# The scale of V in a fused attention and gated-MLP kernel: maximum over partitions through DRAM and VectorE in place of TensorE

## The chip, the cores and the metric

The kernel runs on one NeuronCore of one Trainium2 chip. The metric is the device time of one execution in microseconds; 649.65 us is the median of three runs of the kernel before (648.05 to 651.03). The engines are named as in the profile: PE is TensorE's matmuls and PEld its weight loads, DVE is VectorE, ACT is ScalarE, POOL is GpSimd, and SP is the engine whose queue issues every DMA of this kernel. Each engine takes its instructions strictly in the order in which the program put them.

## The reference, cut to what matters

Eight batches, eight heads, 576 positions, head dimension 64, float32. Attention looks back at most 127 positions, so a tile of 128 queries meets two tiles of 128 keys.

```python
scores = scale * np.matmul(q, k.transpose(0, 1, 3, 2))
scores = np.where(mask, scores + bias[None], -1000000000.0)   # 0 <= i - j < 128, a slope per head
attn = np.exp(scores - max)
attn = attn / (sum + 1e-09)
out = np.matmul(attn, v)
x = out.transpose(0, 2, 1, 3).reshape(B, S, H * D)
h = np.maximum(x @ w_in, 0.0)
u, v = h[..., :512], h[..., 512:]
v_n = (v - mu) / np.sqrt(var + 1e-06)
v_s = w_spatial @ v_n + b_spatial
return (u * v_s) @ w_out
```

## The kernel before, in words

Work comes in blocks and units. An attention block is one batch and two heads, 32 blocks in all; five of them (batch 0 and the first of batch 1) run in another way, `raw_tile`, and are not touched. The other 27 run in `attention`: scores on PE (L520: eight matmuls for the first four query tiles, then two for the last; the profile counts each of these float32 matmuls twice), bias and minimum on DVE (L531), exponential with row sums on ACT (L537), a reciprocal (L545, L549), two float16 halves of the probabilities (L557 on ACT, L562 on DVE), one DMA transpose for each head (L568, on SP), and probabilities times V on PE in float16 (L624, 84 matmuls). ACT and DVE then copy the result out of PSUM as two float32r parts (L633, L637), with a small copy of the last 64 columns (L267).

For the float16 product V is scaled by a power of two and split into `vh` and `vl`. The scale comes from the largest row sum of |V|: ACT takes the sums of 128 partitions (L579, into column 0 of `am`; its wide output goes to `vl`, which is free then). PE transposes the 128 sums into one row (L583), DVE takes the maximum and clamps it (L587, L588), and PE spreads it to all partitions by two matmuls of one column with constant powers of two (L593). DVE reads the two columns from PSUM and keeps their exponents (L599, L600). Column 5 of `am` then scales V (L604 on DVE or L607 on ACT, and L611), column 6 scales the result back (L633, L637).

The gated MLP of a batch is made of units of one PSUM tile each: v units (L689, 12 matmuls of 512 columns; L711 for the last 64 positions), with a layer norm behind them (L650 to L700); u units (L741, 12 matmuls of 288 columns), spatial units (L762, 14) with L770 and L776 on DVE behind them, and output units (L788, 12) with a copy (L267) and a store (L798). All their matmuls are float32r; those of L520 and L583 are float32, L593 is bfloat16, L624 float16. The tiles `m` of these units have two buffers, the tiles `x` (L624's result, and the little tile `mp` of L583 and L593) two, `vh`, `vl` and `am` two.

The order on every engine is written by a planner (class `Plan`). Every operation has an engine, an estimated length and a due time; the planner runs these through a list schedule with a fixed latency for each engine (2200 ns for a DMA) and emits the program in that order. So an operation with other estimates moves others, on every engine. The attention blocks of a batch stand among the units of the batch before.

Of the kernel before, what the change touches and what calls it, by code (L numbers as in the profile page):

```python
# [9 lines left out]
F32 = mybir.dt.float32  # L10
F32R = mybir.dt.float32r
BF16 = mybir.dt.bfloat16
F16 = mybir.dt.float16
I32 = mybir.dt.int32
U32 = mybir.dt.uint32
AF = mybir.ActivationFunctionType
ALU = mybir.AluOpType
AX = mybir.AxisListType
# [120 lines left out]
def attn_gmlp_kernel(ctx, tc, qk, v, w_in, w_spT, b_sp, w_out, outT):  # L139
# [3 lines left out]
    nc = tc.nc  # L143
    B, H, D, _, S = qk.shape
    P = 2 * D
# [22 lines left out]

    const = ctx.enter_context(tc.tile_pool(name="const", bufs=1))
    work = ctx.enter_context(tc.tile_pool(name="work", bufs=2))  # L170
    ps = ctx.enter_context(tc.tile_pool(name="ps", bufs=1, space=PSUM))
    ctx.enter_context(tc.manual_schedule())
    plan = Plan()

    def fixed(shape, dtype, name):
        t = const.tile(shape, dtype, name=name)
        return Buf(lambda: t)

    def dve(n, fast=False):
        return 75 + n / (1.92 if fast else 0.96)  # L180
# [13 lines left out]

    nhalf = fixed([P, 1], F32, "nhalf")
    ident = fixed([P, P], F32, "ident")
    ones = fixed([1, 2 * P], BF16, "ones")
    tabs = [fixed([P, 2 * P], BF16, f"tab{h}") for h in range(H)]
    win = fixed([P, NC_, 2, DF], F32R, "win")
    wout = fixed([P, ND, 2, DM], F32R, "wout")  # L200
# [23 lines left out]
    def constants():  # L224
        def f():
            nc.gpsimd.iota(relf(), [[-1, 2 * P]], base=P, channel_multiplier=1, allow_small_or_imprecise_dtypes=True)
        plan.add("POOL", 400, 0, f, (), [(relf, 0)])

        def f():
            nc.vector.memset(maskt(), 0.0)  # L230
        plan.add("DVE", dve(256), 0, f, (), [(maskt, 0)])

        def f():
            nc.gpsimd.affine_select(maskt(), maskt(), [[-1, 2 * P]], ALU.is_ge, MASKED, base=P, channel_multiplier=1)
            nc.gpsimd.affine_select(maskt(), maskt(), [[1, 2 * P]], ALU.is_ge, MASKED, base=-1, channel_multiplier=-1)
        plan.add("POOL", 800, 1, f, [(maskt, 0)], [(maskt, 0)])

        def f():
            nc.vector.memset(ident(), 1.0)
            nc.vector.memset(ones()[:, :P], 2.0 ** -12)  # L240
            nc.vector.memset(ones()[:, P:], 2.0 ** -13 / PSC)
            nc.vector.memset(nhalf(), -0.5)
            nc.vector.memset(rstat(), 1.0)
        plan.add("DVE", dve(400), 500, f, (), [(ident, 0), (ones, 0), (nhalf, 0)] + [(rstat, k) for k in range(8)])

        def f():
            nc.gpsimd.affine_select(ident(), ident(), [[-1, P]], ALU.is_ge, 0.0, base=0, channel_multiplier=1)
            nc.gpsimd.affine_select(ident(), ident(), [[1, P]], ALU.is_ge, 0.0, base=0, channel_multiplier=-1)
        plan.add("POOL", 600, 500, f, [(ident, 0)], [(ident, 0)])

        def f():
            nc.vector.tensor_scalar(minus(), ident(), -1.0, None, ALU.mult)
        plan.add("DVE", 150, 501, f, [(ident, 0)], [(minus, 0)])
        for j in range(2):
            def f(j=j):
                nc.vector.memset(stat[j](), 1.0)
            plan.add("DVE", dve(64), 600, f, (), [(stat[j], x) for x in range(99)])
        for h in range(H):
            def f(h=h):
                slope = 2.0 ** (-8.0 * (h + 1) / H)  # L260
                nc.vector.scalar_tensor_tensor(tabs[h](), relf(), -8.0 * slope, maskt(), ALU.mult, ALU.add)
            plan.add("DVE", dve(256), 1000 + h * 4000, f, [(relf, 0), (maskt, 0)], [(tabs[h], 0)])
# [237 lines left out]
    def attention(b, p):  # L500
# [70 lines left out]

        vh, vl = (plan.buf(work, tag, 2, [P, NQ, P], F16) for tag in ("vh", "vl"))
        am = plan.buf(work, "am", 2, [P, 8], F32)
        one = plan.buf(work, "one", 2, [1, 2], BF16)
        mp = plan.buf(ps, "x", 2, [P, 512], F32)
        d = due - 3000

        def f():
            nc.scalar.activation(vl(), vr(), AF.Abs, accum_out=am()[:, 0:1])  # L579
        plan.add("ACT", act(NQ * P, 1), d, f, VRS, [(vl, 0), (am, 0)])  # L580

        def f():
            nc.tensor.transpose(mp()[0:1, 0:P], am()[:, 0:1], ident())  # L583
        plan.add("PE", SWITCH // 2, d + 1, f, [(am, 0), (ident, 0)], [(mp, 0)])

        def f():
            nc.vector.tensor_reduce(one()[:, 0:1], mp()[0:1, 0:P], AX.X, ALU.max)  # L587
            nc.vector.tensor_scalar(one()[:, 0:1], one()[:, 0:1], 2.0 ** -98, 2.0 ** 126, ALU.max, ALU.min)  # L588
        plan.add("DVE", 400, d + 2, f, [(mp, 0)], [(one, 0)])

        def f():
            for k in range(2):
                nc.tensor.matmul(mp()[:, P + k:P + k + 1], ones()[:, k * P:(k + 1) * P], one()[:, 0:1], start=True, stop=True,  # L593
                                 skip_group_check=True)
        plan.add("PE", SWITCH, d + 3, f, [(one, 0), (ones, 0)], [(mp, 1)])

        def f():
            bits = 0x7F800000
            nc.vector.tensor_scalar(am()[:, 5:7].bitcast(I32), mp()[:, P:P + 2].bitcast(I32), bits, None, ALU.bitwise_and)  # L599
            nc.vector.tensor_scalar(am()[:, 5:6].bitcast(I32), am()[:, 5:6].bitcast(I32), bits, None, ALU.bitwise_xor)  # L600
        plan.add("DVE", 150, d + 4, f, [(mp, 1)], [(am, 1)])

        def fv():
            nc.vector.tensor_scalar(vh(), vr(), am()[:, 5:6], None, ALU.mult)  # L604
# [268 lines left out]
```

## Time and profile before

| What | Value |
|---|---|
| Runs | 648.05, 651.03, 649.65 us; median 649.65 us |
| Profiled execution | 648.05 us |
| Its span, first to last instruction | 646.3 us |
| Granted TensorE clock, mean | 0.992 |
| PE busy | 619.0 us (96%) |
| DVE busy | 524.2 us (81%) |
| ACT busy | 430.9 us (67%) |
| One batch in the steady part (375.78 to 448.74 us) | 72.96 us |

Busy time of PE is the time in which some matmul was under way; matmuls are pipelined, so a group's length says less than the distance from its start to the start of what follows. Rows of the timeline give the start, the length, the engine, the line, the operation, the tiles and the count; in brackets stands the idle time before it and what ended it.

### The profile page before, as it was taken

What the parts mean: (1) busy time and instruction counts of PE and PEld (TensorE: products, weight loads), DVE (VectorE), ACT (ScalarE), POOL (GpSimd) and SP (SyncE); (2) the same over time, 40 slices, a digit from 0 to 9 for tenths busy, and PEclk for the clock granted to TensorE, in tenths of its full rate; (3) what the DMA queues carried; (4) which work ended last, traced back from release to release, by engine and by line L of the source; (5) the groups of instructions that cost most, each with busy time, mean ns of one, the idle gap of its engine ahead of it and who ended that gap; (6) DMA issues with size and microseconds to landing.
All of it is one profiled execution on the core that took longest, in us unless ns stands there. A gap on an engine that the chain in (4) does not pass through costs nothing.

```text
span 646.3 us, 14141 instructions
## 1 busy us (share of the span) xinstructions
PE 619.0 (96%) x5037; PEld 529.8 (82%) x5037; DVE 524.2 (81%) x1897; ACT 430.9 (67%) x1322; POOL 29.6 (5%) x53
## 2 busy tenths in 40 slices
PE   4879999999999999999999999999999999999997
PEld 2445688778899879988898979988898978988997
DVE  6999898999887979887887979887887979873632
ACT  4698675989585848686686848676686857662211
POOL 1000010000200010000100010000100010000100
PEclk9998799999999999999999999999999999999999
DMA  7903013799156863778165753858166751733001
GB/s 264 329 20 130 19 62 119 169 209 202 55 132 133 190 107 93 155 155 184 40 143 127 191 112 89 154 152 188 32 154 125 193 113 10 132 79 76 2 20 55
DMA packets 149291, 79.34 MB, mean 123 GB/s; under 512 B 128610, under 2 KB 139874, under 8 KB 149220
## 3 DMA queue, kind: packets, MB, share of 16 engines
q1 hardware_dynamic: 149220, 78.44, 51.8%
q8 instruction: 39, 0.64, 0.4%
q14 instruction: 32, 0.26, 0.1%
HBM read 37.13 MB, written 9.44 MB: 72 GB/s over the span
## 4 chain that ended last, share of the span: by engine, by line
PE 79%; DVE 17%; issue 1%; DMA 1%; ACT 1%; SPq 1%; ACTq 0%; DVEq 0%
PE m L762 16%; PE m L741 16%; PE m L788 14%; PE m L689 13%; PE s L520 8%; PE x L624 6%; DVE pq L562 4%; PE m L711 2%; DVE prob L436 2%; DVE prob L531 2%; DVE gs L298 1%; DMA pt<-in_qk_dram 1%; DVE prob L450 1%; DVE u L770 1%; DVE o L267 1%
## 5 line engine op out<-in xcount | busy, mean ns | idle before, releaser
L537 ACT ACTIVATE prob<-prob,stat 128x128 f32<-128x128 f32 (+1 forms) x270 | 125.4, 466 | 13.6 <-DVE stat L531 12.4
L762 PE MATMUL m<-wsp,vn 128*128 128x288 f32 x768 | 124.3, 299 | 0.7 <-DVE u L770 0.7
L788 PE MATMUL m<-gs,wout 128*128 128x288 f32 x768 | 113.5, 301 | 0.3 <-DVE gs L776 0.2
L762 PEld LDWEIGHTS m<-wsp,vn 128*128 128x128 f32 x768 | 107.5, 188 | 6.7 <-issue 1.9
L557 ACT ACTIVATE pq<-prob,stat 128x128 f16<-128x128 f32 x270 | 103.1, 464 | 12.7 <-ACT prob L537 10.2
L741 PE MATMUL m<-xt,win 128*128 128x288 f32 x768 | 111.6, 298 | 0.0
L788 PEld LDWEIGHTS m<-gs,wout 128*128 128x128 f32 x768 | 103.3, 188 | 7.2 <-issue 1.7
L562 DVE SCALAR_TENSOR_TENSOR pq<-prob,stat,pq 128x128 f16<-128x128 f32 x270 | 104.0, 437 | 4.3 <-ACT pq L557 3.7
L741 PEld LDWEIGHTS m<-xt,win 128*128 128x128 f32 x768 | 103.9, 188 | 4.1 <-issue 2.3
L689 PE MATMUL m<-win,xt 128*128 128x512 f32 x384 | 93.5, 396 | 1.7 <-DVE o L267 1.7
L531 DVE CUSTOM_DVE_ANT_0 prob<-s,tab 128x128 f32<-128x128 f32 (+1 forms) x270 | 89.2, 376 | 2.6 <-PE s L520 2.1
L689 PEld LDWEIGHTS m<-win,xt 128*128 128x128 f32 x384 | 71.5, 189 | 18.2 <-DVE o L267 2.8
L520 PE MATMUL s<-qkraw 64*128 64x256 f32 (+2 forms) x540 | 66.5, 360 | 1.5 <-DVE stat L531 1.3
L770 DVE TENSOR_TENSOR u<-m,u 128x288 f32<-128x288 f32 x64 | 28.9, 451 | 34.2 <-PE m L762 34.2
L520 PEld LDWEIGHTS s<-qkraw 64*128 64x128 f32 (+1 forms) x540 | 42.0, 175 | 16.2 <-issue 9.0
L659 POOL TENSOR_TENSOR st<-st,nhalf 128x1 f32<-128x1 f32 (+1 forms) x40 | 25.6, 640 | 560.4 <-DVE st L655 548.0
L537 ACT ACTIVATION_READ_ACCUMULATOR prob<-prob,stat 128x1 f32 x270 | 50.6, 187 | 0.0
L267 ACT COPY o<-m 128x288 f32<-128x288 f32 x37 | 14.6, 395 | 46.2 <-PE m L788 45.9
L624 PE MATMUL x<-pt,vh 128*64 128x256 f16 (+6 forms) x756 | 41.7, 229 | 0.0
L271 ACT ACTIVATE vt<-m 128x512 f32<-128x512 f32 x31 | 18.5, 598 | 33.0 <-DVE st L654 16.1
L637 DVE SCALAR_TENSOR_TENSOR xt<-x,am,xt 128x288 fp32r<-128x288 f32 x54 | 26.2, 507 | 17.1 <-ACT xt L633 17.0
L624 PEld LDWEIGHTS <-vh 128*64 128x64 f16 x756 | 31.7, 110 | 5.8 <-issue 3.5
(132 smaller groups left out, 820.7 us busy)
## 6 DMA issues: line engine op xcount, KB each, us to landing
qkraw<-in_qk_dram SPq DMA_DIRECT2D x28, 576.0 KB, 3.9
out_dram<-o SPq DMA_DIRECT2D x64, 144.0 KB, 2.0
vraw<-in_v_dram SPq DMA_DIRECT2D x28, 320.0 KB, 2.9
vn<-in_w_in_dram SPq DMA_DIRECT2D x6, 512.0 KB, 7.1
pt<-in_w_out_dram SPq DMA_DIRECT2D x4, 512.0 KB, 4.5
gs<-in_w_spT_dram SPq DMA_DIRECT2D x4, 288.0 KB, 5.0
xt<-in_w_in_dram SPq DMA_DIRECT2D x2, 512.0 KB, 6.8
qkraw<-in_qk_dram SPq DMA_DIRECT2D x3, 320.0 KB, 8.3
```

The costliest lines, as they stand in the source:

```text
L520: nc.tensor.matmul(sc[k][j]()[:m, i, :k1 - k0], raw()[rows, 0, t * P:t * P + m], raw()[rows, 1, k0:k1], start=True, stop=True)
L531: nc.vector.tensor_tensor_reduce(pt(), sc()[:m, i, :n], tabs[h]()[:m, c0:c0 + n], -0.125, 3e38, ALU.add, ALU.min, st()[:m, NM, j, t:t + 1])
L537: nc.scalar.activation(pt(), pt(), AF.Exp, bias=st()[:m, NM, j, t:t + 1], scale=-1.0, accum_out=st()[:m, SM, j, t:t + 1])
L557: nc.scalar.activation(pq[j]()[:m, 0, cs], prob[j]()[:m, cs], AF.Copy, scale=st()[:m, RC, j, t:t + 1])
L562: nc.vector.scalar_tensor_tensor(pq[j]()[:m, 1, cs], prob[j]()[:m, cs], st()[:m, RC, j, t:t + 1], pq[j]()[:m, 0, cs], ALU.mult, ALU.subtract)
L624: nc.tensor.matmul(xp()[j * D:(j + 1) * D, x0:x0 + n], l()[:, kt, j * D:(j + 1) * D], rhs[:, o:o + n], start=j not in seen, stop=False, sk ...
L637: nc.vector.scalar_tensor_tensor(xt()[:, S + R + hf * HS:S + R + (hf + 1) * HS], xp()[:, :HS], am()[:, 6:7], xt()[:, qs].bitcast(F32), ALU ...
L689: nc.tensor.matmul(pt(), xt[c]()[:, X0[a] + t * P:X0[a] + (t + 1) * P], win()[:, c, w, DH:DF], start=(n == 0), stop=(n == 3 * NC_ - 1))
L741: nc.tensor.matmul(pt()[:, :HS], win()[:, c, w, d * P:(d + 1) * P], xt[c]()[:, X0[a] + hf * HS:X0[a] + (hf + 1) * HS], start=(n == 0), sto ...
L762: nc.tensor.matmul(pt()[:, :HS], l, r, start=(n == 0), stop=(n == len(ops) - 1))
L770: nc.vector.tensor_tensor(u(), pt()[:, :HS], u(), ALU.mult)
L788: nc.tensor.matmul(pt()[:, :HS], wout()[:, d, w, e * P:(e + 1) * P], gs[d]()[:, a, :], start=(n == 0), stop=(n == 3 * ND - 1))
```

## The change

The row sums go from column 0 of `am` to a DRAM tile of 128 words by one DMA (`row`), and from there to every partition by a second one, a broadcast of 512 bytes to each of 128 partitions, into the first 128 words of `vl` seen as float32. Both are issued on SP; the second waits for the landing of the first. DVE then does the rest on all 128 partitions: maximum, clamp, exponent bits, product with the two powers of two, and the flip of the exponent bits. The transpose, the two matmuls, the tile `mp`, the tile `one` and the constant row `ones` are gone; a constant of two columns (`powers`) takes its place. The arithmetic of the rest is the same.

```diff
+    dram = ctx.enter_context(tc.tile_pool(name="dram", bufs=2, space=bass.MemoryType.DRAM))
...
-            nc.vector.memset(ones()[:, :P], 2.0 ** -12)
-            nc.vector.memset(ones()[:, P:], 2.0 ** -13 / PSC)
+            nc.vector.memset(powers()[:, 0:1], 2.0 ** -12)
+            nc.vector.memset(powers()[:, 1:2], 2.0 ** -13 / PSC)
...
-        def f():
-            nc.tensor.transpose(mp()[0:1, 0:P], am()[:, 0:1], ident())
-        plan.add("PE", SWITCH // 2, d + 1, f, [(am, 0), (ident, 0)], [(mp, 0)])
-
-        def f():
-            nc.vector.tensor_reduce(one()[:, 0:1], mp()[0:1, 0:P], AX.X, ALU.max)
-            nc.vector.tensor_scalar(one()[:, 0:1], one()[:, 0:1], 2.0 ** -98, 2.0 ** 126, ALU.max, ALU.min)
-        plan.add("DVE", 400, d + 2, f, [(mp, 0)], [(one, 0)])
-
-        def f():
-            for k in range(2):
-                nc.tensor.matmul(mp()[:, P + k:P + k + 1], ones()[:, k * P:(k + 1) * P], one()[:, 0:1], start=True, stop=True,
-                                 skip_group_check=True)
-        plan.add("PE", SWITCH, d + 3, f, [(one, 0), (ones, 0)], [(mp, 1)])
+
+        row = plan.buf(dram, "row", 2, [P, 1], F32)
+        wide = lambda: vl().rearrange("p a b -> p (a b)").bitcast(F32)[:, :P]
+
+        def f():
+            nc.sync.dma_start(row(), am()[:, 0:1])
+        plan.add("SP", 60, d + 1, f, [(am, 0)], [(row, 0)])
+
+        def f():
+            nc.sync.dma_start(wide(), row().rearrange("p o -> (p o)").partition_broadcast(P))
+        plan.add("SP", 300, d + 2, f, [(row, 0)], [(vl, 0)])
 
         def f():
             bits = 0x7F800000
-            nc.vector.tensor_scalar(am()[:, 5:7].bitcast(I32), mp()[:, P:P + 2].bitcast(I32), bits, None, ALU.bitwise_and)
+            nc.vector.tensor_reduce(am()[:, 1:2], wide(), AX.X, ALU.max)
+            nc.vector.tensor_scalar(am()[:, 2:3], am()[:, 1:2], 2.0 ** -98, 2.0 ** 126, ALU.max, ALU.min)
+            nc.vector.tensor_scalar(am()[:, 2:3].bitcast(I32), am()[:, 2:3].bitcast(I32), bits, None, ALU.bitwise_and)
+            nc.vector.tensor_scalar(am()[:, 5:7], powers(), am()[:, 2:3], None, ALU.mult)
             nc.vector.tensor_scalar(am()[:, 5:6].bitcast(I32), am()[:, 5:6].bitcast(I32), bits, None, ALU.bitwise_xor)
-        plan.add("DVE", 150, d + 4, f, [(mp, 1)], [(am, 1)])
+        plan.add("DVE", 600, d + 4, f, [(vl, 0), (powers, 0)], [(am, 1)])
```

In the changed kernel lines up to the pool stand where they were; from there to the place of the change they are one higher (L520 is L521), behind it one lower (L624 is L623). The new lines are L586 (`row`), L590 (the broadcast) and L595 to L599 on DVE.

The planner moves the rest. The first place is PE, from the end of a steady batch's attention to the v units of the next batch. Before:

```order
L583 MATMUL x<-ident,am 1x128
L689 MATMUL m<-win,xt 128x512 x12
L593 LDWEIGHTS ones
L593 MATMUL x<-one,ones 128x1
L593 LDWEIGHTS ones
L593 MATMUL x<-one,ones 128x1
L711 MATMUL m<-win,xt 128x512 x8
L689 MATMUL m<-win,xt 128x512 x12
```

Ahead of these rows stand 24 matmuls of L788, and ahead of those the 84 of L624, the last block of the batch. Now (L623 is the last block's product, L521 the scores, L688 and L710 the v units):

```order
L623 LDWEIGHTS vl
L623 MATMUL x<-pt,vl 64x64
L521 MATMUL s<-qkraw 128x128 x2
L521 MATMUL s<-qkraw 128x256 x6
L688 MATMUL m<-win,xt 128x512 x12
L710 MATMUL m<-win,xt 128x512 x8
L688 MATMUL m<-win,xt 128x512 x36
```

The three instructions of the scale are gone here. The first v unit now stands one group of scores behind the product whose result it reads, where two output units stood between them, and three v units stand behind L710 where one did.

The second place is SP in the middle of a steady batch, where the two transposes of that last block are issued. `pq_85` and `pq_86` before, `pq_87` and `pq_88` now, are the same two tiles, one for each head. Before:

```order
L409 DMA qkraw<-in_qk_dram 128x1152
L798 DMA out_dram<-o 128x288
L411 DMA vraw<-in_v_dram 128x640
L568 DMA_TRANSPOSE pt<-pq_85 128x18x128
L568 DMA_TRANSPOSE pt<-pq_86 128x18x128
L409 DMA qkraw<-in_qk_dram 128x1152
```

Now:

```order
L797 DMA out_dram<-o 128x288
L412 DMA vraw<-in_v_dram 128x640
L586 DMA row<-am 128x1
L797 DMA out_dram<-o 128x288
L569 DMA_TRANSPOSE pt<-pq_87 128x18x128
L590 DMA vl<-row 128x128
L569 DMA_TRANSPOSE pt<-pq_88 128x18x128
L797 DMA out_dram<-o 128x288 x2
```

The second transpose now stands behind a DMA that waits for the landing of `row`.

The third place is DVE at the end of a steady batch, ahead of the copies of that block's result (L636 now, L637 before). Now:

```order
L268 COPY o<-m 128x288
L595 TENSOR_REDUCE am<-vl 128x1
L596 TENSOR_SCALAR am<-am 128x1
L597 TENSOR_SCALAR am<-am 128x1
L598 TENSOR_SCALAR am<-powers,am 128x2
L599 TENSOR_SCALAR am<-am 128x1
L532 ISA prob_86,stat_89<-s,tab_72 128x256
L532 ISA stat_89 128x1
L603 TENSOR_SCALAR vh<-vraw,am 128x640
L610 SCALAR_TENSOR_TENSOR vl<-vraw,am,vh 128x640
```

Behind them come L532, L546, L550 and three L563, and then L636. Before, the scale that comes next at this place (L587 and what follows it) stood behind the copies of this block; now a scale's five instructions and the split of another block's V stand ahead of them.

More of the change, by code (lines that the diff above doesn't have):

```diff
@@ L196, in attn_gmlp_kernel @@
     ident = fixed([P, P], F32, "ident")
-    ones = fixed([1, 2 * P], BF16, "ones")
+    powers = fixed([P, 2], F32, "powers")
     tabs = [fixed([P, 2 * P], BF16, f"tab{h}") for h in range(H)]
@@ L239, in f @@
             nc.vector.memset(ident(), 1.0)
-            nc.vector.memset(ones()[:, :P], 2.0 ** -12)
-            nc.vector.memset(ones()[:, P:], 2.0 ** -13 / PSC)
+            nc.vector.memset(powers()[:, 0:1], 2.0 ** -12)
+            nc.vector.memset(powers()[:, 1:2], 2.0 ** -13 / PSC)
             nc.vector.memset(nhalf(), -0.5)
             nc.vector.memset(rstat(), 1.0)
-        plan.add("DVE", dve(400), 500, f, (), [(ident, 0), (ones, 0), (nhalf, 0)] + [(rstat, k) for k in range(8)])
+        plan.add("DVE", dve(400), 500, f, (), [(ident, 0), (powers, 0), (nhalf, 0)] + [(rstat, k) for k in range(8)])
         def f():
@@ L573, in attention @@
         am = plan.buf(work, "am", 2, [P, 8], F32)
-        one = plan.buf(work, "one", 2, [1, 2], BF16)
-        mp = plan.buf(ps, "x", 2, [P, 512], F32)
         d = due - 3000
```

## The prediction

> **What bounds the kernel now.** I read the page first, then one steady batch, then what PE waits for.
>
> ```profile
> span 646.3 us, 14141 instructions
> ...
> PE 619.0 (96%) x5037; PEld 529.8 (82%) x5037; DVE 524.2 (81%) x1897; ACT 430.9 (67%) x1322; POOL 29.6 (5%) x53
> ```
>
> ```profile
> 375.78:448.74 72.96, 72.53 (x621) 63.56 (x621) 61.04 (x223) 52.13 (x164) 3.17 (x5) 1.00 0.58 133
> ...
> 435.00:445.00 10.00, 10.00 (x103) 9.06 (x101) 8.80 (x37) 9.69 (x34) 0.00 (x0) 1.00 0.79 182
> ```
>
> The columns of the second view are length, then busy time of PE, PEld, DVE, ACT and POOL. A steady batch lasts 72.96 us and PE is busy in 72.53 of them; DVE has 11.92 us free. So time taken off PE comes off the batch, as long as nobody makes PE wait. In the ten microseconds ahead of the next batch's v units, though, ACT (9.69 of 10) and DVE (8.80) are nearly full as well: there a delay has the least room. Of PE's own waits the summary has one that returns in every steady batch:
>
> ```profile
> PE m L689 <- DVE o L267: 1.7, 4, 0.4
> ```
>
> **The change: what leaves PE.** The price of a removed group is not its busy time, since matmuls overlap, but the distance between starts. PE in order of time (start, length, then the group):
>
> ```profile
> 423.95 1.86 PE L788 MATMUL m<-gs,wout 128*128 128x288 f32 x12
> 425.65 0.27 PE L583 MATMUL x<-ident,am 128*1 128x128 f32 x1
> 425.85 0.54 PE L520 MATMUL s<-qkraw 64*64 64x192 f32 x4
> 426.32 1.86 PE L788 MATMUL m<-gs,wout 128*128 128x288 f32 x12
> 428.11 0.20 PE L593 MATMUL x<-one,ones 1*128 1x1 bf16 x2
> 428.24 0.66 PE L762 MATMUL m<-wsp,vn 128*128 128x288 f32 x3
> ...
> 435.92 0.88 PE L520 MATMUL s<-qkraw 64*64 64x192 f32 x4
> 436.73 3.44 PE L788 MATMUL m<-gs,wout 128*128 128x288 f32 x24
> 440.10 0.41 PE L624 MATMUL x<-pt,vh 128*64 128x256 f16 x4
> ...
> 441.60 3.44 PE L788 MATMUL m<-gs,wout 128*128 128x288 f32 x24
> 444.88 0.27 PE L583 MATMUL x<-ident,am 128*1 128x128 f32 x1
> 445.58 3.03 PE L689 MATMUL m<-win,xt 128*128 128x512 f32 x12 [0.43 <-DVE o L267]
> 448.55 0.20 PE L593 MATMUL x<-one,ones 1*128 1x1 bf16 x2
> 448.67 2.11 PE L711 MATMUL m<-win,xt 128*128 128x512 f32 x8
> ...
> 460.68 1.79 PE L520 MATMUL s<-qkraw 64*128 64x128 f32 x16
> 462.40 1.85 PE L741 MATMUL m<-xt,win 128*128 128x288 f32 x12
> 464.09 0.27 PE L583 MATMUL x<-ident,am 128*1 128x128 f32 x1
> 464.12 1.84 PE L741 MATMUL m<-xt,win 128*128 128x288 f32 x12
> 465.89 0.54 PE L520 MATMUL s<-qkraw 64*64 64x192 f32 x4
> 466.37 0.20 PE L593 MATMUL x<-one,ones 1*128 1x1 bf16 x2
> 466.49 3.72 PE L741 MATMUL m<-xt,win 128*128 128x288 f32 x26
> ```
>
> The block at 464: L583 takes 0.03, the L741 behind it 1.77 where the one ahead takes 1.69 (0.08 more), L593 0.12: together 0.23. The block at 425: L583 takes 0.20 ahead of L520, L593 0.13, and the L788 that now borders on L593 takes 1.79, where one of the 24 at 436.73 takes 3.37 / 2 = 1.69 (0.10 more): 0.43. So a change of number format at a border costs about 0.1, and a scale in the middle of float32r units pays it more often than one beside L520. The other two blocks of a batch stand like the second (float32r units around L593) and I count them as 0.43. Mean (0.23 + 3 x 0.43) / 4 = 0.38 us, times 27 blocks = **10.3 us off PE**.
>
> The new order also takes two waits from their places. From L583 at 444.88 to L689 are 0.70 us where 0.03 is the price: 0.67 of waiting, 0.43 of it under the name of a copy out of PSUM (the tiles `m` have two buffers). Now other groups stand between that copy and the v unit. It came four times: 2.7 us. The L520 at 435.92 takes 0.81 where the one at 425.85 takes 0.47; it now stands elsewhere: 0.34 in five batches, 1.7 us. Upper bound of the gain: 10.3 + 2.7 + 1.7 = 14.7 us.
>
> **What is added to DVE.** Rows of the grouped view, one execution each:
>
> ```profile
> L587 DVE TENSOR_REDUCE one<-x 1x1 bf16<-1x128 f32 x27 | 7.4, 273 | 0.0
> L588 DVE TENSOR_SCALAR one<-one 1x1 bf16<-1x1 bf16 x27 | 3.9, 145 | 0.9
> L600 DVE TENSOR_SCALAR am<-am 128x1 int32<-128x1 int32 x27 | 4.2, 154 | 0.9
> L599 DVE TENSOR_SCALAR am<-x 128x2 int32<-128x2 int32 x27 | 4.1, 154 | 12.3 <-PE x L593 12.3
> ```
>
> Those rows are 273 + 145 + 154 + 154 = 0.73 us for a block. The new five are one maximum over 128 words (taken as L587's 273 ns) and four small operations (L600's 154 ns): 0.89. That is 0.16 us more for a block, 0.65 in a batch with 11.92 us of DVE idle: nothing by itself, 4.3 us in all if DVE had no idle time left.
>
> **What is added to SP and to the wait.** Issues and landings:
>
> ```profile
> out_dram<-o SPq DMA_DIRECT2D x64, 144.0 KB, 2.0
> pt<-pq SPq DMA_TRANSPOSE x54, 4.7
> ```
>
> ```profile
> 446.06 0.53 SPq L798 DMA_DIRECT2D out_dram<-o  x1
> 446.75 2.71 SPq L568 DMA_TRANSPOSE pt<-pq  x1
> ```
>
> No transfer as small as these two stands in the trace, so I take the store, the nearest: 2.0 us from issue to landing. The pair needs 4.0 us from the sums to the spread row, or more behind a transpose, whose data land 4.7 us after its issue began and 2.0 after it ended. Before, the same path was:
>
> ```profile
> 445.35 0.73 ACT L579 ACTIVATE vl<-vraw 128x640 f16<-128x640 f32 x1
> ...
> 448.65 0.60 ACT L271 ACTIVATE vt<-m 128x512 f32<-128x512 f32 x1 [2.19 <-PE m L689]
> ```
>
> ```profile
> 444.23 0.93 DVE L637 SCALAR_TENSOR_TENSOR xt<-x,am,xt 128x288 fp32r<-128x288 f32 x2
> ...
> 448.78 0.16 DVE L599 TENSOR_SCALAR am<-x 128x2 int32<-128x2 int32 x1 [2.16 <-PE x L593]
> ```
>
> The sums were done at about 446.1 and DVE had them back at 448.8: 2.7 us, 2.16 of it spent idle at L599. The transfers need 1.3 us more at the least. What hides them is the distance that the new order leaves between L579 on ACT and L595 on DVE, which holds other blocks' softmax work. Where it is too short, DVE stands at L595, and behind it in its queue stand the split of V, the softmax of the next block and the copies out of PSUM, for which PE waits in the end. Bounds of such a stand: 0, and 2 us for a block. I count none of it alone, because DVE stood 2.16 us in the middle of that path before without more than the 0.67 on PE; its weight enters below.
>
> SP gets 54 issues of about 0.5 us, 27 us in a span in which it mostly waits for its inputs. But the broadcast's wait for the landing of `row` blocks SP for up to 2 us, and a transpose stands behind it: the second head's transpose of a batch's last block. Its cover is the transpose ahead of it, 2.7 us of issue, in which `row` lands. I take 0.5 us, hidden.
>
> **The wait that moves.** The first v unit reads the result of the block just ahead. Before, that block's L624 began at 440.10 and its L637 ended at 445.16, 5.06 us later; L788 x24 stood between. Now only 1.50 (L624) and 1.72 (the L520 at 460.68) stand there, 3.22 us: 1.84 short. In return the copies come earlier: ahead of L633 on ACT eight L557 had to go,
>
> ```profile
> 440.46 3.04 ACT L557 ACTIVATE pq<-prob,stat 128x128 f16<-128x128 f32 x8 [0.31 <-ACT prob L537]
> ```
>
> and now three do, five of 0.38 fewer, 1.9 us. So the wait is between 0 and 1.8, plus what L595, now ahead of these copies on DVE, is late: I take 0.6 us, a third of the bound, since the earlier start cancels most of it. Five batches: 3.0 us. In the last batch no score group stands between, 1.72 more: 2.0 us. Together **5.0 us given back**.
>
> **Sum.** 10.3 + 2.7 + 1.7 - 5.0 = 9.7 us. The profiled execution took 648.05 us (span 646.3, and 1.75 around it): 638.4. The median of the runs lies 1.6 above the profiled one, so I predict **640 us**. With no wait at the v units it is 635, and with 1.8 in each of six and 2 us of DVE standing behind it, (1.8 + 2) x 6 = 23 us, it would be 658.
>
> **Rivals.**
>
> *All of the gain arrives, and more.* If the copies are ready and PE also loses other idle time at borders (the new order has one island of other formats fewer in a batch, about 0.2 us), the 14.7 us and 1.2 more come off: 649.65 - 15.9 = 634, or less. For it: PE has almost no other wait in the trace. Against: the ten microseconds of the second view, where ACT and DVE are full. Chance 0.15.
>
> *The gain is eaten.* DVE stands at L595 for about 1 us in each batch's end and the v unit waits 1.8: 2.8 x 5 = 14, nothing left, 647 to 651. For it: DVE already stood 2.16 us for the scale, and DMAs are slower than the path through PE. The Trainium skill gives another way to the same end: its page "TensorE: Matmul & The Clock Gate", section "Wait — 56ns, not 53.3ns?", has matmuls at least about 25 ns apart however small; three of them would be 0.075 us in a block and 2 us in all, 648. The L583 at 464.09 agrees with that floor (0.03), but L593's 0.12 and the 0.1 at each border do not, so I give the floor little. Chance 0.18.
>
> *Slower.* SP is the place: a broadcast that waits there holds the transposes behind it, so `pt` comes late and PE stands at L624, which it never did before. It decides where a transpose comes more than about 0.55 us late in each block (14.7 / 27), for the whole gain is spent then; with the full 2.0 us of one landing in half of the blocks the loss is 27 us against 14.7, and the time 662. Against: loads and stores leave SP room, and a transpose's input is mostly what SP waits for. The Trainium skill's "DMA: Bandwidth & Descriptors", section "Anatomy of one DMA — SWDGE (gpsimd) path", says, of a DMA on GpSimd's path, that completion can be surprisingly long where HBM is written, as `row` does; the store's 2.0 us is such a write and is not. Chance 0.14.
>
> **How the numbers follow.** My forecast, faster by a part of the gain (635 to 646), has 0.53; with the first rival that makes 0.68 for faster by over 0.5%. Half a percent is about what a measurement of this kernel can tell from no change, 646.4 to 652.9 here: 0.18. Slower: 0.14. The range leaves out a part of the slower case and the far end of the best: 631 to 653; the forecast's own is 634 to 646.
>
> **What would show it.** L583 and L593 gone, a steady batch of about 71 us (72.96 less 1.5 for the scales, less 0.67 and 0.34, plus 0.6), and the groups around the old places 0.1 us shorter each: the PE price is right. A wait of the first v unit (now L688) for L636 of some tenths of a microsecond: the moved wait is right; over 1.8, L595 is in it. L595's idle time should be under 1 us a block, `row` and the broadcast should land 2 us after their issue, and L623 should wait for no transpose. A `row` that lands after 4 us or more, or a batch that stays at 73 us, proves the forecast wrong.

## The result and the profile after

| | Before | After |
|---|---|---|
| Median of the runs | 649.65 us (648.05 to 651.03, three runs) | 787.2 us (777.51 to 792.11, four runs) |
| Ratio after / before | | 1.207, 95% interval 1.192 to 1.222 |
| Profiled execution, span | 648.05, 646.3 us | 786.25, 784.5 us |
| Granted TensorE clock, mean | 0.992 | 0.917 |

One more run before, of 1167.1 us, and the longest of the four after are slow ones and do not enter the ratio; without the latter the median after is 786.25 us. The changed kernel is 21% slower, where 640 us was predicted. The page of the changed kernel, its first lines and then the group of the new maximum:

```profile
span 784.5 us, 14132 instructions
...
PE 655.6 (84%) x4956; PEld 563.9 (72%) x4956; DVE 537.4 (68%) x1936; ACT 429.0 (55%) x1310; POOL 29.3 (4%) x53
...
L595 DVE TENSOR_REDUCE am<-vl 128x1 f32<-128x128 f32 x27 | 7.7, 285 | 132.1 <-DMA vl<-row 90.9
```

PE has 81 matmuls fewer and is nevertheless busy for longer, and idle for 784.5 - 655.6 = 128.9 us where it was idle for 27.3. DVE stands idle ahead of L595 for 132.1 us, 4.9 for each of 27 blocks. The DMA view of the same kernel (kilobytes, then the median time from issue to landing, over those DMAs whose landing the trace holds):

```profile
out_dram<-o SPq DMA_DIRECT2D x64, 144.0 KB, 2.2
...
vl<-row SPq DMA_DIRECT2D x27, 64.0 KB, 4.4
...
pt<-pq SPq DMA_TRANSPOSE x54, 5.5
...
row<-am SPq DMA_DIRECT2D x27, 0.5 KB, 8.1
```

The smallest of these transfers takes longest: `row` moves 512 bytes and lands after 8.1 us; a store of 144 KB lands after 2.2. The trace holds few of these landings (2 of 27 for `row`, 3 of 27 for the broadcast, 3 of 64 stores), but the timeline has every issue: from the issue of `row` to that of the broadcast, which waits for its landing, are 7.6 to 10.5 us, 8.7 in the median of all 27. The 128 packets of four bytes of `row` are not what takes the time. Those of the `row` issued at 366.36 us were all under way between 367.40 and 367.59 us, 7 to 9 ns each, and its landing was seen nearly 7 us later. The waits of SP's queue, DVE and PE (total, times, longest):

```profile
SPq L590 <- DMA row<-am: 142.5, 24, 8.3
```

```profile
DVE am L595 <- DMA vl<-row: 90.9, 21, 9.7
DVE am L595 <- issue: 41.2, 4, 10.9
```

```profile
PE m L740 <- DVE vt L273: 29.2, 5, 6.9
PE m L761 <- DVE o L268: 24.0, 6, 4.4
PE s L521 <- DVE stat L532: 16.0, 8, 3.4
PE m L761 <- ACT o L268: 12.8, 5, 3.5
```

SP stands at the broadcast for the landing of `row`, DVE at L595 for the landing of the broadcast, and PE for the copies and the softmax that are queued behind L595. For four of DVE's 25 stands (41.2 us) the profile names no releaser; but they end 5.0 to 5.3 us after the issue of the broadcast that they read, and the 21 others 3.1 to 5.4 us after it. ACT stands as well, 61.4 us ahead of the 13 splits of V that it does (L606), for the result of L599. PE does not name the transfer, and for the transposes of the probabilities it waits only 4.8 us in all. One such passage in the timeline, all engines:

```profile
366.36 0.53 SPq L586 DMA_DIRECT2D row<-am  x1
...
374.25 0.33 SPq L590 DMA_DIRECT2D vl<-row  x1
...
378.48 0.29 DVE L595 TENSOR_REDUCE am<-vl 128x1 f32<-128x128 f32 x1 [4.69 <-DMA vl<-row]
...
380.57 0.68 DVE L273 TENSOR_SCALAR vt<-m 128x512 f32<-128x512 f32 x1
...
381.31 8.40 PE L740 MATMUL m<-xt,win 128*128 128x288 f32 x48 [4.89 <-DVE vt L273]
```

7.89 us for `row`, 4.23 for the broadcast. DVE has run out of other work 4.69 us before that; behind L595 stands L273, the copy that empties a PSUM tile, and PE needs that tile: 4.89 us of waiting on PE.

The lost time has a second part. The stretches around that wait (length, busy time and count of PE, PEld, DVE, ACT, POOL, then the granted clock, DMA share, GB/s):

```profile
366.00:376.00 10.00, 10.00 (x85) 8.23 (x86) 6.77 (x18) 4.07 (x8) 2.42 (x4) 1.00 0.18 35
376.00:381.30 5.30, 0.41 (x4) 0.06 (x3) 2.68 (x9) 1.67 (x4) 0.00 (x0) 0.73 0.43 124
381.30:384.00 2.70, 2.69 (x11) 2.69 (x12) 2.70 (x5) 1.74 (x5) 0.00 (x0) 0.50 0.01 0
384.00:388.00 4.00, 4.00 (x28) 4.00 (x27) 3.08 (x15) 2.73 (x10) 0.55 (x1) 0.85 0.87 26
388.00:392.00 4.00, 4.00 (x32) 4.00 (x32) 3.85 (x11) 2.64 (x8) 0.00 (x0) 1.00 0.68 33
```

The clock was 1.00 before PE's wait, 0.50 in the 2.7 us behind it, 0.85 on average in the next four, and 1.00 again after that. So this stand of PE is paid once as idle time and again as slower matmuls. The Trainium skill's page "TensorE: Matmul & The Clock Gate", section "HAM oscillation — how this bites in real kernels", warns of gaps on PE above about 3.4 us, behind which matmuls start at half the clock; this trace agrees, with 4.89 us and 0.50. Here waits below the page's figure had the same result too: 0.50 in the 2.7 us behind waits of 2.53 us (up to 354.96) and 2.99 us (up to 399.87), though not behind every one (1.00 behind 2.83 us, up to 427.31).

### The profile page after: what moved, and what is told of

It is laid out like the page before. It is cut to its first block, busy times and chain, and to the rows that moved or that the text cites. A ratio compares the mean times of both kernels' runs of the same rounds, so it can differ in the third digit from the quotient of the medians.

```text
span 784.5 us, 14132 instructions
## 1 busy us (share of the span) xinstructions
PE 655.6 (84%) x4956; PEld 563.9 (72%) x4956; DVE 537.4 (68%) x1936; ACT 429.0 (55%) x1310; POOL 29.3 (4%) x53
## 5 line engine op out<-in xcount | busy, mean ns | idle before, releaser
L761 PE MATMUL m<-wsp,vn 128*128 128x288 f32 x768 | 140.2, 326 | 42.5 <-DVE o L268 24.0
L761 PEld LDWEIGHTS m<-wsp,vn 128*128 128x128 f32 x768 | 123.0, 214 | 50.8 <-DVE o L268 25.5
L740 PE MATMUL m<-xt,win 128*128 128x288 f32 x768 | 123.0, 319 | 33.8 <-DVE vt L273 29.2
L740 PEld LDWEIGHTS m<-xt,win 128*128 128x128 f32 x768 | 116.9, 210 | 37.6 <-DVE vt L273 30.9
L563 DVE SCALAR_TENSOR_TENSOR pq<-prob,stat,pq 128x128 f16<-128x128 f32 x270 | 104.7, 434 | 6.2 <-ACT pq L558 5.6
L688 PE MATMUL m<-win,xt 128*128 128x512 f32 x384 | 98.0, 408 | 7.1 <-DVE o L268 4.2
L595 DVE TENSOR_REDUCE am<-vl 128x1 f32<-128x128 f32 x27 | 7.7, 285 | 132.1 <-DMA vl<-row 90.9
L688 PEld LDWEIGHTS m<-win,xt 128*128 128x128 f32 x384 | 73.1, 195 | 29.8 <-ACT vt L272 6.1
L532 DVE CUSTOM_DVE_ANT_0 prob<-s,tab 128x128 f32<-128x128 f32 (+1 forms) x270 | 89.0, 374 | 7.8 <-PE s L521 7.3
L521 PE MATMUL s<-qkraw 64*128 64x256 f32 (+2 forms) x540 | 69.3, 372 | 16.1 <-DVE stat L532 16.0
L521 PEld LDWEIGHTS s<-qkraw 64*128 64x128 f32 (+1 forms) x540 | 43.8, 182 | 29.2 <-DVE stat L532 19.8
L623 PE MATMUL x<-pt,vh 128*64 128x32 f16 (+6 forms) x756 | 45.2, 236 | 5.0 <-DMA pt<-pq 4.8
L606 ACT ACTIVATE vh<-vraw,am 128x640 f16<-128x640 f32 x13 | 10.8, 828 | 61.4 <-DVE am L599 61.4
L623 PEld LDWEIGHTS <-vh 128*64 128x64 f16 x756 | 34.8, 114 | 11.5 <-issue 11.5
```

The lines of the kernel that those rows point to most:

```text
L521: nc.tensor.matmul(sc[k][j]()[:m, i, :k1 - k0], raw()[rows, 0, t * P:t * P + m], raw()[rows, 1, k0:k1], start=True, stop=True)
L532: nc.vector.tensor_tensor_reduce(pt(), sc()[:m, i, :n], tabs[h]()[:m, c0:c0 + n], -0.125, 3e38, ALU.add, ALU.min, st()[:m, NM, j, t:t + 1])
L563: nc.vector.scalar_tensor_tensor(pq[j]()[:m, 1, cs], prob[j]()[:m, cs], st()[:m, RC, j, t:t + 1], pq[j]()[:m, 0, cs], ALU.mult, ALU.subtract)
L623: nc.tensor.matmul(xp()[j * D:(j + 1) * D, x0:x0 + n], l()[:, kt, j * D:(j + 1) * D], rhs[:, o:o + n], start=j not in seen, stop=False, sk ...
L688: nc.tensor.matmul(pt(), xt[c]()[:, X0[a] + t * P:X0[a] + (t + 1) * P], win()[:, c, w, DH:DF], start=(n == 0), stop=(n == 3 * NC_ - 1))
L740: nc.tensor.matmul(pt()[:, :HS], win()[:, c, w, d * P:(d + 1) * P], xt[c]()[:, X0[a] + hf * HS:X0[a] + (hf + 1) * HS], start=(n == 0), sto ...
```

## The experiments

The theory after the result: the landing of `row` is slow; the work taken off PE is worth what was forecast; what costs is the wait for the landing, in two places, SP's queue and DVE's. The first rival: the new order on the engines is bad by itself. The second: SP's hold delays transposes and stores, and DVE's stand matters little. Single times below come from one profiled execution; ratios come with an interval. The kernel before took 648.66 to 650.9 us beside these runs (medians of seven runs, or single ones).

### The new order without the transfers

```diff
-            nc.sync.dma_start(row(), am()[:, 0:1])
+            pass
-            nc.sync.dma_start(wide(), row().rearrange("p o -> (p o)").partition_broadcast(P))
+            pass
-            nc.vector.tensor_scalar(am()[:, 2:3], am()[:, 1:2], 2.0 ** -98, 2.0 ** 126, ALU.max, ALU.min)
+            nc.vector.tensor_scalar(am()[:, 2:3], am()[:, 1:2], 32.0, 32.0, ALU.max, ALU.min)
```

> The changed kernel with the two transfers left out and its order kept on every engine; the maximum over partitions is thereby left out too, the scale comes from a constant 32 (the clamp's both ends). If DVE's stand at L595 for the transfers is the whole loss (137 us), the time falls to 630 to 645 us, L595's idle time from 132 us to under 10, and this shows what PE gains without the three tiny groups: a steady batch of 70 to 71 us. If the new order itself costs (the wait of the v unit for the copies, up to 1.8 us a batch and what DVE adds), the time is 645 to 660 us and PE waits at L688 and L740. If something else of the change is slow, it stays above 700 us.

Measured: 640.79 us, ratio to before 0.986 (0.983 to 0.988). Two steady batches by window, same columns as above:

```profile
304.43:375.53 71.10, 70.99 (x609) 63.04 (x608) 62.97 (x231) 51.14 (x162) 3.06 (x5) 1.00 0.61 136
375.53:446.62 71.09, 71.00 (x609) 63.06 (x608) 62.98 (x231) 51.17 (x162) 3.07 (x5) 1.00 0.62 136
```

A batch of 71.1 us in place of 72.96, PE busy 71.00 in place of 72.53. The first rival falls: order, DVE's longer chain and the shorter PE are together worth about what was forecast (9.2 us by the medians beside each other, 649.97 and 640.79). The whole loss, 787.2 - 640.8 = 146 us, comes with the two transfers. The page of this kernel, its first lines and then the group of the v units:

```profile
span 639.8 us, 14004 instructions
...
PE 612.4 (96%) x4956; PEld 528.7 (83%) x4956; DVE 534.7 (84%) x1936; ACT 427.0 (67%) x1310; POOL 29.3 (5%) x53
...
L688 PE MATMUL m<-win,xt 128*128 128x512 f32 x384 | 94.2, 399 | 0.0
```

PE is busy for 612.4 us with the same 4956 matmuls that take 655.6 in the changed kernel. Of the 144.7 us between the two spans (784.5 and 639.8), 43.2 are slower matmuls (the mean granted clock is 0.917 and 0.986) and 101.5 are idle time on PE.

### The transfers beside the old path

```diff
+        row = plan.buf(dram, "row", 2, [P, 1], F32)
+        wide = plan.buf(work, "wide", 2, [P, 16], F32)
+
+        def f():
+            nc.sync.dma_start(row(), am()[:, 0:1])
+        plan.add("SP", 60, d + 1, f, [(am, 0)], [(row, 0)])
+
+        def f():
+            nc.sync.dma_start(wide(), row()[0:16].rearrange("p o -> (p o)").partition_broadcast(P))
+        plan.add("SP", 300, d + 2, f, [(row, 0)], [(wide, 0)])
```

This is added to the kernel before; nobody reads `wide`.

> The kernel before with its path through PE, and beside it the two transfers on the same queue at the same place of the plan; the broadcast (16 of the words, 64 bytes a partition) goes to a scratch tile that nobody reads. Theory, DVE's stand is the loss: nobody waits for these transfers, the time stays within 1.5% of before (640 to 660 us), although SP waits 5 to 8 us a block for the landing of row. Rival, SP's hold is a large part of the loss: transposes and loads behind it come late, PE waits at L624 and DVE or ACT for its inputs, 680 us or more. Row should land after about 8 us here too.

Measured: 707.66 us, 58 above before. The theory of this expectation (640 to 660 us) falls, and its rival, SP's hold, stands. No computing engine waits for these transfers, so this is what they do to SP's queue and to the other DMAs:

```profile
out_dram<-o SPq DMA_DIRECT2D x64, 144.0 KB, 4.5
...
pt<-pq SPq DMA_TRANSPOSE x54, 5.3
row<-am SPq DMA_DIRECT2D x27, 0.5 KB, 8.9
```

```profile
PE x L636 <- DMA pt<-pq: 19.6, 10, 3.2
```

SP stood 118.7 us at the broadcast. PE waited for transposes, as the predicted slower case had it; that is 19.6 of the 42.8 us that it stood idle longer than in the kernel before (70.1 and 27.3), and the other waits were not followed up. The stores whose landing the trace holds (17 of 64) landed after 4.5 us where they took 2.0 before; whether the slow writes slow them in the memory or only shift them against other traffic was not separated.

### Both transfers, and DVE does not wait

```diff
-            nc.sync.dma_start(wide(), row().rearrange("p o -> (p o)").partition_broadcast(P))
+            nc.sync.dma_start(apart[p % 2](), row()[0:16].rearrange("p o -> (p o)").partition_broadcast(P))
-            nc.vector.tensor_scalar(am()[:, 2:3], am()[:, 1:2], 2.0 ** -98, 2.0 ** 126, ALU.max, ALU.min)
+            nc.vector.tensor_scalar(am()[:, 2:3], am()[:, 1:2], 32.0, 32.0, ALU.max, ALU.min)
```

> The changed kernel in its own order on every engine, with both transfers, but the broadcast (16 words, 64 bytes a partition) goes to a scratch tile, so that DVE's L595 waits for no DMA; the maximum is left out and the scale comes from a constant 32. It leaves the transfers and SP's hold and takes DVE's stand away. Theory after the run with transfers beside the old path (58 us more than before): hold and slowed transfers are a part, 40 to 70 us, so 680 to 710 us here, with PE waiting for transposes and DVE for stores; the rest of the 146 us between this order without transfers (641) and the change (787), some 80 to 105 us, is DVE's stand. Rival, the stand is all of it: 640 to 655 us. Rival, the hold is all of it: 770 us or more.

Measured: 682.97 us. SP waits as long as in the changed kernel:

```profile
SPq L591 <- DMA row<-am: 142.3, 24, 7.8
```

So of the 146 us about 42 (683.0 - 640.8) go with SP's hold and the other DMAs, and about 104 (787.2 - 683.0) with DVE's stand at L595. The second rival names a real cost, but the smaller one. The broadcast is of 64 bytes a partition here and of 512 in the changed kernel; its landing is 4.7 us here and 4.4 there (3 of 27 landings each), so the split does not seem to hang on that. The shares hold for this order of taking the costs away; a kernel with DVE's stand and without SP's hold was not run.

### The planner told the latency

```diff
+                    end += self.late.get(n, 0)
-        plan.add("SP", 60, d + 1, f, [(am, 0)], [(row, 0)])
+        plan.add("SP", 60, d + 1, f, [(am, 0)], [(row, 0)], 6000)
-        plan.add("SP", 300, d + 2, f, [(row, 0)], [(vl, 0)])
+        plan.add("SP", 300, d + 2, f, [(row, 0)], [(vl, 0)], 2000)
```

> The changed kernel with the planner told of 6000 ns more until row has landed and 2000 ns more for the broadcast, so that DVE's L595 comes later in its order; nothing else is edited. If DVE's stand comes from the planner's 2200 ns alone, the order hides it and what is left is SP's hold and the slowed transfers: 680 to 710 us, L595 idle under 30 us in all. If the plan can't hide it (the split of V is needed soon after), it stays above 740 us.

Measured: 712.09 us, 2 above the expected range. The planner puts other work into the gaps, and DVE's stand is nearly gone (12.2 us for the broadcast), SP's hold is 28.6 us, but the wait goes elsewhere:

```profile
PE x L625 <- DMA pt<-pq: 24.6, 12, 4.6
```

Transposes land after 6.4 us and PE waits for them; that is a third of PE's 710.4 - 630.5 = 80 us of idle time, and the rest was not followed up. This order wins back half of the loss; whether another would win more, no run shows.

### Why `row` is slow: distance, size and number of the words

A DRAM tile with one word in each 512 bytes:

```diff
+    rows = [(lambda t: Buf(lambda: t))(dram.tile([P, P], F32, name=f"row{i}")) for i in range(2)]
...
+                nc.sync.dma_start(rows[i](), ident())
...
-        row = plan.buf(dram, "row", 2, [P, 1], F32)
+        row = rows[p % 2]
...
-            nc.sync.dma_start(row(), am()[:, 0:1])
+            nc.sync.dma_start(row()[:, 0:1], am()[:, 0:1])
...
-            nc.sync.dma_start(wide(), row().rearrange("p o -> (p o)").partition_broadcast(P))
+            nc.sync.dma_start(wide(), row()[0].partition_broadcast(P))
```

> The changed kernel with each of the 128 words of row written 512 bytes from the next, in a DRAM tile of 128 x 128 words that is filled once at the start; the broadcast reads 512 bytes in one piece as before, of which only the first word is new, so the maximum is taken over one partition's sum alone. Theory, 128 writes of 4 bytes into the same 512 bytes of DRAM take their turns (6.6 us / 128 = 52 ns each): row lands in 2 to 2.5 us in place of 8.1, and the time falls by 27 x 4 to 27 x 5.6 us at most, to 650 to 700. Rival, every 4-byte write to DRAM is late wherever it goes, or the wait is for the transposes ahead in the queue: row still takes about 8 us, and the time stays at 770 to 790.

512 bytes from every partition (`row` of 128 x 128 words, written from `wide`), and the maximum replaced by a constant:

> The changed kernel with 512 bytes written from every partition (64 KB, from the tile that holds the wide output of the sums) in place of 4; the broadcast reads the first row; the maximum is left out, the scale comes from a constant 32. Theory and the rival of small writes both have row land in 2.0 to 2.5 us and the time at 650 to 700 us, as in the run with words 512 bytes apart or a little less; if the landing waits for transposes or for the issue itself, it stays at about 8 us and 770 to 790 us.

Half of the words (`row()[0:64]`, `wide()[:, :64]`):

> The changed kernel with 64 of the 128 words: the sums of partitions 0 to 63 alone are written, spread and searched, so the maximum leaves out the other half. Theory, writes into the same 512 bytes take turns: with 8.1 us for 128 words and 2.0 us where none share (words 512 bytes apart), half of the words take 2.0 + 6.1 / 2 = 5.0 us to land; the time falls to about 700 to 730 us. Rival, a fixed delay of small writes to one place (a page or a buffer that is busy for 6 us whatever the count): row lands after 8 us, 775 to 790 us.

The first two answered alike: 2.0 and 2.1 us for `row`, 651.67 and 644.68 us for the kernel. So neither the size nor the number of pieces makes `row` slow; what is left is that the words lie close together, or that the tile of the first run was fixed, which a control below tests. The third missed its number: 7.2 us where turn-taking word by word gave 5.0, and 733.67 us. So the latency is not in proportion to the number of words. Three runs with other distances and numbers followed. Their edit is that of the run with 512 bytes, with tiles of 16 and 4 words a partition, and that of the half with `[0:16]`:

> The 128 words are written 64 B apart into a DRAM tile that was filled at the start; the broadcast reads its first 512 B, so the maximum is taken over the sums of the first 8 partitions only. With words 4 B apart the row took 8.1 us, with words 512 B apart 2.0 us. Theory A (the writes take turns within a line of DRAM of 64 B or less, lines go side by side): the row takes 2.0 us again, and the kernel about 650 us as with 512 B. Theory B (the turns are taken within a piece of 512 B or a larger area): 8 writes fall in each 512 B, the row takes 5 to 8 us and the kernel 700 us or more.

> The words are written 16 B apart; the broadcast reads the first 512 B, so the maximum is taken over the sums of the first 32 partitions. Theory A: 4 writes fall in each 64 B; from 2.0 us for one and 8.1 us for sixteen, that is 0.41 us for each further write, so 2.0 + 3 x 0.41 = 3.2 us, and the kernel between 650 and 680 us. Theory B: 32 writes in each 512 B, 7 to 8 us and over 720 us.

> Only the words of partitions 0 to 15 are written, 4 B apart, 64 B in all, and only they are broadcast and enter the maximum. Theory A: one line takes all 16 turns, so the row takes about 7 us, as with 64 and 128 words (7.2 and 8.1), and the kernel stays above 700 us. Theory C (what counts is the number of small writes, 8.1 us for 128): 2.0 + 16/128 x 6.1 = 2.8 us, and the kernel about 650 us.

All three were quick: 2.1, 2.1 and 2.0 us for `row`. So each theory of these expectations fell somewhere. A, turns within 64 bytes, gave 3.2 us for the words 16 bytes apart, and fell on the last, since sixteen words in 64 bytes cost nothing; B, larger pieces, fell as it was put, since 8 and 32 writes in 512 bytes cost nothing; C, the mere number of writes, had the last right, but 128 writes landed in 2.1 us in the two before it. Three more runs closed in on it, one of them a control, because the runs with a distance also kept their tiles fixed and filled them once:

> The DRAM tiles are fixed and filled at the start, as in the runs with words apart, but the words are 4 B apart again; the maximum is over all partitions. If the distance made those runs quick, this one is slow as the changed kernel: row 7 to 8 us and 760 to 790 us. If the fixed tiles made them quick, the row takes 2.0 us and the kernel about 650 us.

> 128 words 8 B apart, 1 KB in all; the broadcast reads the first 512 B, so the maximum is over the first 64 partitions. Theory D (what counts is how many writes fall into one piece of 256 or 512 B: slow with 64, quick with 16): 32 in 256 B, between the two known cases, so a row between 2.1 and 7.2 us. Theory E (only neighbours that touch, 4 B apart and in number, are slow): 2.0 to 2.1 us and about 650 us.

> Only the words of partitions 0 to 31, 4 B apart, 128 B in all, are written, broadcast and enter the maximum. 16 such words took 2.0 us, 64 took 7.2. Theory D: 32 writes in a piece of 256 B, as with the words 8 B apart, and so the same row time as there. Theory E: they touch, so slow like 64 words, 5 to 7 us, while the words 8 B apart are quick.

The control is slow, so the fixed tiles are not what helps. The DMA row of the kernel with words 512 bytes apart, and those of the last three kernels in the order above:

```profile
row<-am SPq DMA_DIRECT2D x27, 0.5 KB, 2.0
```

```profile
row<-am SPq DMA_DIRECT2D x27, 0.5 KB, 7.5
```

```profile
row<-am SPq DMA_DIRECT2D x27, 0.5 KB, 3.8
```

```profile
row<-am SPq DMA_DIRECT2D x27, 0.1 KB, 4.1
```

The table has the median landing, with the number of landings (of 27) that the trace holds, and the median time from the issue of `row` to that of its broadcast, over all 27.

| Run | Words, distance | Writes in 256 B | `row`, us (landings) | Issue to issue, us | Kernel, us |
|---|---|---|---|---|---|
| changed kernel | 128, 4 B | 64 | 8.1 (2) | 8.7 | 787.2 |
| control, fixed tile | 128, 4 B | 64 | 7.5 (1) | 8.1 | 779.2 |
| half of the words | 64, 4 B | 64 | 7.2 (19) | 7.3 | 733.7 |
| 32 words | 32, 4 B | 32 | 4.1 (24) | 4.3 | 676.4 |
| 8 B apart | 128, 8 B | 32 | 3.8 (24) | 3.9 | 666.5 |
| 16 words | 16, 4 B | 16 | 2.0 (24) | 2.1 | 644.0 |
| 16 B apart | 128, 16 B | 16 | 2.1 (24) | 2.1 | 650.3 |
| 64 B apart | 128, 64 B | 4 | 2.1 (24) | 2.2 | 650.1 |
| 512 B apart | 128, 512 B | 1 | 2.0 (24) | 2.1 | 651.7 |

The latency goes with the number of separate writes that fall into one piece of DRAM, and 256 bytes is the piece that orders the table, if the fullest piece alone counts: by 128 bytes, 32 writes would have to cost both 8.1 us (changed kernel) and 4.1 (32 words); by 512 bytes, 64 would cost both 7.2 (half) and 3.8 (8 B apart). Up to 16 writes hide in the 2.0 us of a quick row; 64 cost 7.2 to 8.1 us, by this estimate 0.11 to 0.13 us each. The broadcast that reads the words back rises in the same order: 2.9 us at 1 and 4 writes, 3.5 and 3.6 at 16, 3.7 and 4.6 at 32, 4.1 to 4.9 at 64 (8 to 64 KB, by the number of words that a run spreads). Theory E of the last runs (only neighbours that touch) falls with the 3.8 us of the words 8 bytes apart. What in the memory takes the turns, and where its pieces begin, no run shows. The Trainium skill's "DMA: Bandwidth & Descriptors", section "Specifications", gives 512 bytes as the smallest transfer at line rate, with a read-modify-write below it; here single words 16 bytes apart land in 2.1 us like pieces of 512 bytes, so being small is not enough to be slow. The kernels with fixed tiles and a quick `row` stand 5 to 9 us above the others of equal `row`; one early batch of theirs holds some 5 us more (76.5 to 76.9 us, where the kernel of the next section has 71.9), and their later steady batches agree with that kernel's within 1.4 us. Why that batch is longer was not followed up.

### A transpose on DVE, and four pieces in place of 128

```diff
-        row = plan.buf(dram, "row", 2, [P, 1], F32)
+        row = plan.buf(dram, "row", 2, [4, 32], F32)
+        quad = lambda: vl().rearrange("p a b -> p (a b)").bitcast(F32)[:, P:P + 32]
+
+        def f():
+            nc.vector.transpose(quad(), am()[:, 0:1].to_broadcast([P, 32]))
+        plan.add("DVE", 150, d + 1, f, [(am, 0)], [(vl, 0)])
-            nc.sync.dma_start(row(), am()[:, 0:1])
+            nc.sync.dma_start(row(), quad()[0:P:32])
```

The transpose works on blocks of 32 partitions and 32 columns here, so 32 sums come to lie side by side in one partition, and the row is written as four pieces of 128 bytes. Nothing is left out.

> The changed kernel with one more DVE instruction: a transpose of 32 x 32 blocks puts the 32 sums of each quarter of the partitions into one row, so that row is written by 4 pieces of 128 bytes in place of 128 of 4 bytes; the broadcast, the maximum and the rest are as in the change, nothing is left out. Theory: 4 writes into the same 512 bytes take 2.0 us and 4 x 0.05, row lands in 2.0 to 2.4 us, and the time is that of the run with 512 bytes of each partition (644.7) and 0.2 us of DVE a block: 642 to 650 us, less than the kernel before. Rival, any several writes to one place are slow: row above 4 us, 670 us or more.

Measured: 642.49 us, ratio to before 0.988 (0.986 to 0.990). The median lies below both kernels; the kernel without transfers and with a constant scale is only 1.7 us faster. The waits of DVE and of SP's queue, and one pair of issues:

```profile
DVE am L600 <- DMA vl<-row: 6.8, 6, 2.0
```

```profile
SPq L595 <- DMA row<-vl: 19.8, 17, 1.9
```

```profile
379.68 0.61 SPq L591 DMA_DIRECT2D row<-vl  x1
381.96 0.34 SPq L595 DMA_DIRECT2D vl<-row  x1
```

DVE stands 6.8 us in place of 132.1, SP 19.8 in place of 142.5, and the broadcast is issued 2.28 us behind `row` here, 2.0 in the median of all 27 pairs. The trace of this kernel holds no landing of `row`, so these distances alone put it at about 2.0 us. The extra operation takes 0.20 us on DVE for a block. With the wait short, the change gives about the gain that was predicted.

## Why the prediction was wrong, step by step

- **PE's price** (0.38 us for a block, 1.5 for a batch): about right. PE's busy time in a steady batch falls from 72.53 to 71.00 us without the transfers, 1.53. That figure is not the price of the scales alone, since part of the two waits below (0.24 of the 0.67, all of the 0.34) stood in PE's busy time as well. The remark that a scale among float32r units pays more does not follow from its rows: in both blocks one of the two groups borders on L520. The fall of busy time over the whole profiled executions, 619.0 to 612.4 us, is smaller, with a mean clock of 0.992 and then 0.986.
- **The waits that lose their place, and 5.0 us given back at the v units**: the batch came out right (72.96 - 71.10 = 1.86 us, where the working has 1.5 + 0.67 + 0.34 - 0.6 = 1.91), but two of its terms came to nothing and cancel in part, which is luck. The 0.34 was saved at its place and lost at others: the four small groups of L520 took 0.48, 0.47, 0.47 and 0.81 us from start to next start, and without the transfers they take 0.63, 0.71, 0.47 and 0.47. The 0.6 was not given back: the v units have no idle time ahead of them in that run (the last column of the line of L688). The sum without the transfers was 640 and 640.8 was measured.
- **DVE's 0.16 us more for a block, hidden**: right as far as the run without transfers shows; its DVE has 71.10 - 62.97 = 8.1 us free in a batch.
- **The price of `row`, the step that failed.** "No transfer as small as these two stands in the trace, so I take the store, the nearest: 2.0 us". A store of 144 KB is near in direction and far in form: it writes long pieces, and `row` writes 64 words into each 256 bytes. `row` took 8.1 us; the broadcast took 4.4, where 2.0 was assumed for it too. So the pair needed 12.1 us from issue to L595 in the passage above, in place of 4.0. The bounds from the store's row were no bounds, since nothing in the trace of before limits a landing from above. Of the sentence in the Trainium skill's "DMA: Bandwidth & Descriptors", section "Anatomy of one DMA — SWDGE (gpsimd) path", that completion can be surprisingly long where HBM is written, the prediction said that the store speaks against it. The runs bear it out for `row`, on SP's queue: the packets of the one followed above were done about 1.2 us after the issue, and the landing of the median one came at 8.1. They do so for close words alone; words 16 bytes apart go to the same memory and land after 2.1 us.
- **DVE's stand at L595, "0, and 2 us for a block", none counted**: it was 4.9 us for a block, and follows from the step before. With about 2 us for `row` (the last experiment) it is 6.8 us over all 27 blocks together, so counting none was near the truth for the price assumed.
- **SP's hold, "0.5 us, hidden"**: 142.5 us at the broadcast, worth about 42 us of time in this order, 58 in the old one.
- **The rivals.** The slower case had the side right and the right trigger, a late landing, but it put the loss on transposes that SP holds and priced it at 662. PE waited only 4.8 us for transposes in the changed kernel. The larger part was the mechanism of "the gain is eaten", DVE at L595, which was priced at 1 us for a batch's end. Neither had a price for the clock: slower matmuls make up 43 of the 145 us.
- **What would show it**: "a `row` that lands after 4 us or more" was named as the proof against the forecast, and is what the profile shows.

## What to carry to other kernels

Price a small transfer by its form, not only by its direction: count the separate writes that fall into each 256 bytes of DRAM, and gather on chip first when there are many (16 cost nothing here, 32 cost 2 us more); one DVE transpose of 0.2 us brought the broadcast's issue from 8.7 to 2.0 us behind that of `row`. Where a DMA in a queue waits for another DMA's landing, give that landing its own upper bound, and follow it into everything that is queued behind the wait on SP and behind its reader. A wait of PE of some 5 us, and here some of 2.5 to 3, costs its length and then several microseconds of matmuls at a lower clock.

## What the runs showed of the hardware that was not expected

- 128 words of four bytes, written side by side into DRAM, land 8.1 us after the issue, while the packets of the one followed were done within 1.3 us of it; spread 16 bytes apart, the same words land after 2.1 us.
- The cost rises with the writes within 256 bytes: 2.0 to 2.1 us up to 16 writes, 3.8 and 4.1 at 32, 7.2 to 8.1 at 64.
- After 4.89 us in which PE stood, its granted clock was 0.50 for 2.7 us and 0.85 on average for the next four; 0.50 also followed waits of 2.53 and 2.99 us.
- The broadcast that reads close words back is slower too: 4.4 us in the changed kernel (3 landings), 2.8 behind four pieces of 128 bytes (6 landings), the same 64 KB in both. A slow `row` is not needed for it: behind a `row` of 2.1 us with words 16 bytes apart it took 3.6 us, again 64 KB.
